# A fused attention, RWKV and expert kernel: attention chunks of 32 queries with two heads side by side, another place for the expert loads, two row buffers

## The chip, the cores and the metric

The kernel runs on one core of a Trainium2 chip. A core has TensorE (PE: matmuls; its weight loads are shown as PEld), VectorE (DVE), ScalarE (ACT), GpSimd (POOL) and SyncE (SP, which issues most DMAs). The metric is the device time of one execution in microseconds; less is better.

## The reference, cut

Three layers follow one another on 2 sequences of 768 tokens. The first is attention with 8 heads of 64, in chunks of 32 queries:

```python
chunk, left_ctx, right_ctx = (32, 16, 8)
for c in range(nc):
    l_start = max(0, c_start - left_ctx); r_end = min(S, c_end + right_ctx)
    k_full = np.concatenate([mem_k, k[:, :, l_start:r_end]], axis=2)   # 8 memory keys first
    scores = scale * np.matmul(q_c, k_full.transpose(0, 1, 3, 2))
    a = softmax(scores)
    out[:, :, c_start:c_end] = np.matmul(a, v_full)
```

So a chunk has at most 8 + 16 + 32 + 8 = 64 keys. The second layer (RWKV channel mixing) mixes each row of 512 with the row before it, and computes `r * v` with `k = relu(xk @ w_k)`, `v = k*k @ w_v`, `r = sigmoid(xr @ w_r)`. The third picks one of 8 experts for each token (a gate decides whether it keeps the expert of the token before), and gives `p[e] * (relu(x @ w1[e]) @ w2[e])`, with w1 512 x 1024 and w2 1024 x 512.

## The kernel before

**Units.** Tokens go in four units of 384. A unit has eight heads, that is four pairs; pairs are numbered 0 to 15 over all units, so pairs 0 to 3 belong to unit 0. The attention of unit u+1 runs between the RWKV matmuls of unit u. The first stage (0 to 98.6 us) is an exception: it splits the weights w_k, w_r and w_v into high and low parts on VectorE, ScalarE and GpSimd, does the attention of units 0 and 1, and the RWKV matmuls of unit 0. Its order is written by hand, as a table of step numbers (`ORDER`, `first_unit`). The later units are ordered by due times (`att_group`, `rwkv_block`, `route_*`).

**Attention.** A score group (`att_s`) is one head of one pair: two small matmuls of a mask from the constants tile `c_sb` (L359, L360), then six matmuls (L364), each of 64 queries against 96 keys, into one bank of PSUM. `att_max` (L372, L373) takes the maximum of each query, `att_exp` (L379) or `att_ex` (L389, first unit) the exponentials on ScalarE, `att_t` (L437) three transposes into a bank, and a copy makes `PT`. In the first stage `att_pvn` (L402) multiplies with the values, `att_nm` (L410 to L412) divides by the sum on VectorE, and `att_xt` (L418) transposes the result. From unit 2 on, `att_rc` (L428, L429) and `att_norm` (on GpSimd) divide before the transposes, and `att_pv` (L453) gives the result already transposed. There are two banks for scores, one (bank 5) for results, and two (6 and 7) for the router.

**RWKV and router.** The 128x384 matmuls of L514 to L516 are RWKV's (three for each product, of high and low parts). The router's matmuls are L602, L613, L645 (transposes of rows), L656 and L688. 

**Experts.** After the router, `tab_a` to `tab_e` (L976 to L1054) build tables of slots on VectorE: which tokens (`gix`, `six`), which expert (`ei`), and whether the slot's expert differs from the last one's. `tab_c` (L1020) multiplies with the last of them, `Rt` (L1008, L1009). A full slot has 128 tokens of one expert, a half slot 64. Full slots split the expert's weights into high and low parts (`w_part`, on ScalarE L863 and VectorE L866), and multiply: `tx` L906, `s1` L915 to L917, `th` L928, `s2` L937 to L939, `put` L942. Here there are 11 full slots (0 to 3, 4 to 7, 8, and 9 and 10 have one expert each), and a half slot follows on slots 3, 5, 7, 8 and 9 (L1111 to L1149), with weights of its own. `w_fetch(s, k)` (L885 to L887) loads the expert's w1 or w2 into the raw buffer if slot s begins a new expert; in the loop it is called as `w_fetch(s + 1, 1)` and `w_fetch(s + 2, 0)`. `h_fetch` (L1098, L1099) loads a half slot's weights. All of these loads are issued by SyncE, one after the other.

**Rows.** `put(s)` scales slot s's result into `ot[0]` on ScalarE; `store()` (L946), called in the next slot, writes it to DRAM by an indirect DMA with the indices `sixl`, which GpSimd copies. `half_rest` at the end is a nest of conditions for half slots that are left over; every engine walks through it.

Of the kernel before, what the change touches and what calls it, by code (L numbers as in the profile page):

```python
# [40 lines left out]
NSLOT = NFULL + NE  # L41
YW = DM + 1
NEGBIG = -float(2.0 ** 99)
# [24 lines left out]
)  # L68
BANKS = {"mm": (0, 1), "S": (2, 3), "pt": (4,), "x": (5,), "mi": (6, 7), "mm0": (0, 1, 6), "S0": (2, 3), "pt0": (4, 7)}


def first_unit_steps():
# [3 lines left out]
    room = dict(S=len(BANKS["S0"]), mm=len(BANKS["mm0"]), pt=len(BANKS["pt0"]), x=1, Pm=3, PT=4, tmp=4, dif=2, wcv=3)  # L76
# [5 lines left out]
    for n in range(8):  # L82
        step(f"qk{n}", "load_qk", (n,), [(DMA, 1.4, "")], (n > 5 and f"S{2 * n - 11}", n and f"qk{n - 1}"))
        step(f"v{n}", "load_v", (n,), [(DMA, 1.3, "")], (n > 2 and f"pv{n - 3}", n and f"v{n - 1}"))
    for n in range(8, 11):
        if n < 10:
            step(f"qk{n}", "load_qk", (n,), [(DMA, 1.4, "")], (f"S{2 * n - 11}", f"qk{n - 1}"))
        step(f"v{n}", "load_v", (n,), [(DMA, 1.3, "")], (f"pv{n - 3}", f"v{n - 1}"))
# [10 lines left out]
    for g in range(2 * H):  # L99
        n = g // 2  # L100
        step(f"S{g}", "att_s", (g,), [(PE, 0.8, "")], (f"qk{n}", f"S{g - 1}" if g else "cst"), take="S")
        step(f"mx{g}", "att_max", (g,), [(DVE, 0.65, "")], (f"S{g}",))
        step(f"ex{g}", "att_ex", (g,), [(ACT, 0.72, "")], (f"mx{g}",), take="Pm", give="S")
        step(f"t{g}", "att_t", (g,), [(PE, 0.33, "")], (f"ex{g}",), take="pt", give="Pm")
        step(f"pt{g}", "att_pt", (g,), [(ACT, 0.38, "a"), (DVE, 0.45, "d")], (f"t{g}",), take="PT", give="pt")
        if g % 2:
            step(f"pv{n}", "att_pvn", (n,), [(PE, 0.75, "")], (f"pt{g - 1}", f"pt{g}", f"v{n}", n and f"pv{n - 1}"),
                 take="x", give="PT PT")
            step(f"nm{n}", "att_nm", (n,), [(DVE, 0.85, "")], (f"pv{n}",), take="tmp", give="x")
            step(f"xt{n}", "att_xt", (n,), [(PE, 0.33, "")], (f"nm{n}",), take="pt", give="tmp")  # L110
            step(f"x{n}", "att_xc", (n,), [(ACT, 0.38, "a"), (DVE, 0.45, "d")], (f"xt{n}", n and f"x{n - 1}"), give="pt")
# [37 lines left out]
def kernel(  # L149
# [23 lines left out]
    banks = [psum.tile([P, 512], F32, name=f"bank{i}") for i in range(8)]  # L173
    turn = dict.fromkeys(BANKS, 0)
    spare = {}

    def bank(tag):

        if tag in spare:
            return banks[spare[tag].pop(0)]  # L180
        of = BANKS[tag]
        turn[tag] += 1
        return banks[of[turn[tag] % len(of)]]
# [36 lines left out]
    c_sb = cp.tile([P, 352], F32, name="c_sb")  # L220
# [9 lines left out]
    hi64 = c_sb[:, 136:137]  # L230
    pcol1 = c_sb[:, 158:159]
# [97 lines left out]
    NG = NU * H  # L329
    Sb, mxs, Pm, sm, PT, pts, xb = {}, {}, {}, {}, {}, {}, {}  # L330
    xT = {}

    def get_xT(u):
        if u not in xT:
# [7 lines left out]
    stock["Pm"] = [(ap_.tile([P, NTI, KW], F32, bufs=1, name=f"Pm{k}"), ap_.tile([P, NTI], F32, bufs=1, name=f"sm{k}"))  # L342
                   for k in range(3)]
    stock["PT"] = [ap_.tile([KW, UT], F32, bufs=1, name=f"PT{k}") for k in range(4)]

    def scores(g):
        return Sb[g][:, 0:NTI * KW].rearrange("p (i k) -> p i k", k=KW)

    def att_s(g):
        n, j = divmod(g, 2)  # L350
        Sb[g] = bank("S0" if g < 2 * H else "S")
        s3 = scores(g)


        o = 32 if n // (H // 2) % 2 == 0 else 64
        m = c_sb[o:o + NCK, 192:352].bitcast(BF16)
# [9 lines left out]
        if j == 1 and 8 <= n < NG // 2 - 2:  # L366
            load_qk(n + 2)
# [961 lines left out]
```

## Time and profile before

| what | value |
|---|---|
| median of 3 runs | 480.97 us (480.62 to 481.92) |
| profiled execution | 480.1 us, of it 478.3 us span of the instructions |
| PE busy | 443.8 us, 93% |
| DVE, ACT, POOL busy | 253.8 (53%), 201.2 (42%), 108.4 us (23%) |
| moved by DMA queues | 73.46 MB, mean 154 GB/s |

The span runs from the first to the last instruction of the profiled execution; 1.8 us lie outside. Busy shares are means over stages of different kinds, so they have to be read by stretches: the first stage to 98.6 us, three units of some 60 us to 283, the experts to 466, and the end.

### The profile page before, as it was taken

The page shows a single profiled execution, that of the slowest core. Times are in us where ns is not written, and L with a number is a line of the kernel's source. Part 1 is how long each engine was busy: PE and PEld are TensorE (multiplying, and loading weights), DVE is VectorE, ACT ScalarE, POOL GpSimd, SP SyncE. Part 2 cuts the span into 40 slices and gives each one's busy share as a digit, 9 for nine tenths or more (in the row PEclk, how much of TensorE's full clock was granted, in tenths as well). Part 3 has the DMA queues.
Part 4 walks back from the last instruction along what each step waited for, and adds up shares of the span by engine and source line. Part 5 has one row for each costly group of instructions (what it writes and reads, how often), then busy time and mean ns, then how long its engine had stood idle before and what let it go on. Part 6 is the DMA issues. An engine that isn't in the chain of part 4 may idle for free. (4 is left out here: it accounts for less than half of the span.)

```text
span 478.3 us, 8826 instructions
## 1 busy us (share of the span) xinstructions
PE 443.8 (93%) x3147; PEld 371.0 (78%) x3147; DVE 253.8 (53%) x659; ACT 201.2 (42%) x486; POOL 108.4 (23%) x121
## 2 busy tenths in 40 slices
PE   1898999999999999999999989998999999989990
PEld 1576899989899898999899967785687786757680
DVE  5999997754754448544960287115342115555120
ACT  2666895346442364422470431225342125555220
POOL 2124210114310144100331611310130120214030
PEclk9999999999999999999999999999899999999996
DMA  8998710102222011000192013999650787991020
GB/s 306 350 320 284 284 53 26 51 6 105 68 69 67 26 67 27 0 1 2 44 346 73 0 46 126 383 398 368 234 207 24 284 304 264 407 344 53 23 77 22
DMA packets 27582, 73.46 MB, mean 154 GB/s; under 512 B 3819, under 2 KB 3951, under 8 KB 27520
## 3 DMA queue, kind: packets, MB, share of 16 engines
q1 hardware_dynamic: 24704, 64.23, 38.0%
q0 software_dynamic: 2816, 8.47, 5.2%
q8 instruction: 30, 0.49, 0.4%
q14 instruction: 32, 0.26, 0.2%
HBM read 106.24 MB, written 6.69 MB: 236 GB/s over the span
## 5 line engine op out<-in xcount | busy, mean ns | idle before, releaser
L899 DVE TENSOR_TENSOR w<-bank,w 128x512 fp32r<-128x512 f32 x34 | 23.4, 688 | 73.6 <-ACTq L877 59.3
L514 PE MATMUL bank<-xkh,w 128*128 128x384 f32 x128 | 46.6, 364 | 0.0
L514 PE MATMUL bank<-k2h,w 128*128 128x384 f32 x128 | 44.8, 350 | 0.0
L866 DVE TENSOR_TENSOR w<-raw,w 128x512 fp32r<-128x512 f32 x56 | 35.8, 696 | 16.0 <-ACT w L863 15.6
L516 PE MATMUL bank<-xkh,w 128*128 128x384 f32 x128 | 43.8, 342 | 0.0
L515 PE MATMUL bank<-xkl,w 128*128 128x384 f32 x128 | 43.7, 342 | 0.0
L516 PE MATMUL bank<-k2h,w 128*128 128x384 f32 x128 | 43.0, 336 | 0.0
L515 PE MATMUL bank<-k2l,w 128*128 128x384 f32 x128 | 42.8, 335 | 0.0
L898 ACT ACTIVATE w<-bank 128x512 fp32r<-128x512 f32 x34 | 20.3, 597 | 49.0 <-PE bank L928 27.3
L207 POOL TENSOR_TENSOR k2l<-tmp,k2h 128x384 fp32r<-128x384 f32 x24 | 26.7, 1114 | 51.5 <-DVE k2h L204 29.4
L863 ACT ACTIVATE w<-raw 128x512 fp32r<-128x512 f32 x64 | 35.3, 620 | 4.5 <-DMA raw<-in_w_dram 4.1
L915 PE MATMUL bank<-w,w 128*128 128x512 f32 x88 | 36.1, 411 | 0.5 <-issue 0.5
L937 PE MATMUL bank<-w,w 128*128 128x512 f32 x88 | 36.4, 414 | 0.0
L939 PE MATMUL bank<-w,w 128*128 128x512 f32 x88 | 34.7, 394 | 0.0
L917 PE MATMUL bank<-w,w 128*128 128x512 f32 x88 | 34.5, 392 | 0.0
L916 PE MATMUL bank<-w,w 128*128 128x512 f32 x88 | 34.4, 391 | 0.0
L938 PE MATMUL bank<-w,w 128*128 128x512 f32 x88 | 34.4, 390 | 0.0
L379 ACT ACTIVATE Pm<-bank,mx 128x96 f32<-128x96 f32 x48 | 15.7, 338 | 26.7 <-DVE mx L373 26.7
L514 PEld LDWEIGHTS bank<-xkh,w 128*128 128x128 f32 x128 | 24.5, 191 | 2.8 <-issue 1.9
L364 PE MATMUL bank<-qk 64*64 64x96 f32 x384 | 26.7, 280 | 0.0
L573 DVE SCALAR_TENSOR_TENSOR yT<-yT,bank 128x384 f32<-128x384 f32 x16 | 8.9, 553 | 31.6 <-PE bank L516 31.6
L514 PEld LDWEIGHTS bank<-k2h,w 128*128 128x128 f32 x128 | 24.0, 188 | 0.9
(222 smaller groups left out, 1005.5 us busy)
## 6 DMA issues: line engine op xcount, KB each, us to landing
raw<-in_w_dram SPq DMA_DIRECT2D x36, 2048.0 KB
qk<-in_qkx_dram SPq DMA_DIRECT2D x16, 480.0 KB
vt<-in_vx_dram SPq DMA_DIRECT2D x16, 292.5 KB
w<-in_wk_dram SPq DMA_DIRECT2D x8, 512.0 KB
w<-in_wv_dram SPq DMA_DIRECT2D x8, 512.0 KB
ys<-yr SPq DMA_DIRECT2D x12, 256.0 KB
w<-in_wr_dram SPq DMA_DIRECT2D x4, 512.0 KB
raw<-in_w_dram SPq DMA_DIRECT2D x2, 1024.0 KB
```

Source lines behind the costliest of these rows:

```text
L207: (nc.vector if e == "d" else nc.gpsimd).tensor_tensor(out=o, in0=a, in1=b, op=op)
L514: nc.tensor.matmul(o[:, :UT], lhsT=wh, rhs=xh, start=first, stop=False)
L515: nc.tensor.matmul(o[:, :UT], lhsT=wh, rhs=xl, start=False, stop=False)
L516: nc.tensor.matmul(o[:, :UT], lhsT=wl, rhs=xh, start=False, stop=last)
L863: nc.scalar.activation(out=hi, in_=src, func=ACTF.Copy)
L866: lo_on.tensor_tensor(out=lo, in0=src, in1=hi.bitcast(F32), op=ALU.subtract)
L915: nc.tensor.matmul(pb, lhsT=xh[:, sl], rhs=wh, start=(c == 0), stop=False)
L916: nc.tensor.matmul(pb, lhsT=xh[:, sl], rhs=wl, start=False, stop=False)
L917: nc.tensor.matmul(pb, lhsT=xl[:, sl], rhs=wh, start=False, stop=(c == NC - 1))
L937: nc.tensor.matmul(pb, lhsT=hh[:, sl], rhs=wh, start=(c == 0), stop=False)
L938: nc.tensor.matmul(pb, lhsT=hh[:, sl], rhs=wl, start=False, stop=False)
L939: nc.tensor.matmul(pb, lhsT=hl[:, sl], rhs=wh, start=False, stop=(c == NF - 1))
```

## The change

1. Attention works on chunks of 32 queries with exactly 64 keys, laid out by the host, so that no mask is needed. Both heads of a pair go together: 24 matmuls of 64 rows and 32 columns for the scores, head j in bank j of a pair of banks `Sb` (2 and 3; there is one such pair), one maximum, six exponentials of 64 columns, three transposes, and 24 matmuls with the values (65 columns, the last gives the sum) into another pair of banks `xb` (5 and 6). All units divide after that product. There are two buffers each for `Pm` and `PT` (three and four before), and two banks instead of three for the first unit's RWKV. The loads grow from 480 to 576 KB (qk) and from 292.5 to 390 KB (vt) for a pair. `ORDER` is another table, and the step rules (`room`, `step`) are those of pairs.
2. `w_fetch` reads a table `nx` of the next expert, made by `tab_n`, and is called when the present expert's raw weights have been split: for the second expert between `h_fetch(0)` and `h_fetch(1)`.
3. `put(s)` writes `ot[s % 2]`, and VectorE copies the indices into `sixl[s % 2]`; half slots have a tile `oh` of their own; two stores stand at the end instead of one.
4. `half_rest` stands in a condition `nr` (from `tab_r`), which is 0 for this data.

```diff
-BANKS = {"mm": (0, 1), "S": (2, 3), "pt": (4,), "x": (5,), "mi": (6, 7), "mm0": (0, 1, 6), "S0": (2, 3), "pt0": (4, 7)}
+BANKS = {"mm": (0, 1), "pt": (4,), "mi": (7,), "mm0": (0, 1), "pt0": (4, 7)}
...
+    def tiles():
         for i in range(NTI):
             for j in range(2):
...
+                for c in range(P // CHUNK):
+                    yield i, j, i * (P // CHUNK) + c, slice(j * D, (j + 1) * D), slice(c * CHUNK, (c + 1) * CHUNK)
+
+    def att_s(n):
+        for i, j, b, rows, cols in tiles():
+            nc.tensor.matmul(scores[cols, j, i, :], lhsT=qk[n][rows, b * CHUNK:(b + 1) * CHUNK],
+                             rhs=qk[n][rows, UT + b * KW:UT + (b + 1) * KW], start=True, stop=True)
...
+    def att_pvn(n):
+        for i, j, b, rows, cols in tiles():
+            nc.tensor.matmul(xb[cols, j, i * (D + 1):(i + 1) * (D + 1)], lhsT=PT[n][rows, b * CHUNK:(b + 1) * CHUNK],
+                             rhs=vt[n][rows, b, :], start=True, stop=True)
...
+    def att_pair(n, t):
+        at(t, att_s, n)
+        at(t + 0.35, att_max, n)
+        at(t + 0.65, att_ex, n)
+        at(t + 3.0, att_t, n)
+        at(t + 3.2, att_pt, n)
+        at(t + 3.7, att_pvn, n)
+        at(t + 3.8, att_nm, n)
+        at(t + 4.7, att_xt, n)
+        at(t + 4.9, att_xc, n)
...
-        ev = nc.values_load(ei[0:1, 0, s:s + 1], engines=(ET.SP,), min_val=0, max_val=NE - 1)
-        fv = nc.values_load(ei[0:1, 1, s:s + 1], engines=(ET.SP,), min_val=0, max_val=1)
+        ev = nc.values_load(nx[0:1, 0, s:s + 1], engines=(ET.SP,), min_val=0, max_val=NE - 1)
+        fv = nc.values_load(nx[0:1, 1, s:s + 1], engines=(ET.SP,), min_val=0, max_val=1)
...
-        nc.scalar.activation(out=ot[0], in_=banks[2 + s % 2], func=ACTF.Copy, scale=yg[s % 3][:, DM:DM + 1])
...
+        nc.scalar.activation(out=ot[s % 2], in_=banks[2 + s % 2], func=ACTF.Copy, scale=yg[s % 3][:, DM:DM + 1])
+        nc.vector.tensor_copy(sixl[s % 2], six[:, s:s + 1])
...
-        (15.3, gather, 2),
+        (15.3, gather, 2), (15.35, tab_n), (15.4, tab_r),
...
+    banks_of["mi"] = (6, 7)
...
         w_part(s, 3)
-        w_fetch(s + 1, 1)
-        store()
-        nc.gpsimd.tensor_copy(sixl, six[:, s:s + 1])
+        if s > 1:
+            w_fetch(s, 1)
+        store((s - 1) % 2)
...
         w_part(s + 1, 1)
-        w_fetch(s + 2, 0)
+        if s > 0:
+            w_fetch(s + 1, 0)
...
     h_fetch(0)
+    w_fetch(0, 0)
+    w_fetch(0, 1)
     h_fetch(1)
     slots(1)
-    half_rest([s >= NMIN for s in HALF_AT].index(True))
-
-    store()
+    nr = nc.values_load(ei[0:1, 0, NSLOT + 2:NSLOT + 3], min_val=0, max_val=1)
+    with tc.If(nr):
+        half_rest([s >= NMIN for s in HALF_AT].index(True))
+
+    store(1)
+    store(0)
```

On TensorE in unit 1, before: the end of one pair's product, and the scores of the next head (`bank_69` is bank 5, `bank_66` bank 2, `bank_65` one of RWKV's).

```order
L453 MATMUL bank_69<-PT_112,vt_916 64x64
L453 MATMUL bank_69<-PT_114,vt_916 64x64
L359 LDWEIGHTS c_sb
L359 MATMUL bank_66<-c_sb 128x192
L360 LDWEIGHTS c_sb
L360 MATMUL bank_66<-c_sb 128x96
L364 MATMUL bank_66<-qk_603 64x96 x6
L514 MATMUL bank_65<-xkh_116,w_173 128x384
L515 MATMUL bank_65<-xkl_117,w_173 128x384
```

The same place after (here `bank_68` is the pair of banks 5 and 6, `bank_66` the pair 2 and 3, and `bank_69` is bank 7):

```order
L480 MATMUL bank_65<-xkl_115,w_530 128x384
L481 MATMUL bank_65<-xkh_114,w_530 128x384
L388 MATMUL bank_68<-vt_970,PT_106 32x65 x24
L363 MATMUL bank_66<-qk_794 32x64 x24
L621 MATMUL bank_69<-ident,r_uk_1358 8x128 x3
L621 MATMUL bank_68<-ident,r_uk_1358 8x128 x3
L479 MATMUL bank_64<-xkh_108,w_260 128x384
```

The mask is gone, product and scores are one group each for a pair, and the router's transposes (L656 before, L621 after) now stand right behind them, half of them into the bank pair of the product.

On VectorE, in the tables, before: the steps from the tokens' slots to the selection `Rt`.

```order
L995 TENSOR_REDUCE se_3090<-sl_3089 128x36
L996 TENSOR_TENSOR slot<-se_3090,Qall 128x12
L997 TENSOR_TENSOR hf<-slot,se_3090 128x12
L998 SCALAR_TENSOR_TENSOR se_3090<-se_3090,slot 128x12
L1000 TENSOR_TENSOR hf<-hf,se_3090 128x12
L1001 TENSOR_TENSOR slot<-slot,hf 128x12
```

The same steps after (L964 to L970), with those of `tab_n` (L1038 to L1047) and `tab_r` (L1027):

```order
L1038 CAST tmp_146<-ei 1x17
L964 TENSOR_REDUCE se_3300<-sl_3299 128x36
L1039 SCALAR_TENSOR_TENSOR tmp_146<-c_sb,tmp_146 1x17
L1041 TENSOR_TENSOR tmp_146<-ef,tmp_146 1x17
L965 TENSOR_TENSOR slot<-se_3300,Qall 128x12
L1040 TENSOR_SCALAR tmp_146<-tmp_146 1x17
L1047 SCALAR_TENSOR_TENSOR nx<-tmp_146 1x17
L966 TENSOR_TENSOR hf<-slot,se_3300 128x12
L967 SCALAR_TENSOR_TENSOR se_3300<-se_3300,slot 128x12
L1042 TENSOR_TENSOR tmp_147<-tmp_146 1x289
L969 TENSOR_TENSOR hf<-hf,se_3300 128x12
L1027 SCALAR_TENSOR_TENSOR hl<-c_sb,tot 1x8
```

The new steps stand between the old ones, ahead of `Rt`.

On SyncE, after: between the half slots' weights `raw_1` and `raw_2` now stands the load of the next full expert (`raw_0`).

```order
L1095 DMA raw_1_3417<-in_w_dram 128x8x512
L851 TENSOR_LOAD nx
L851 ISA x2
L852 TENSOR_LOAD nx
L852 ISA x2
L853 ISA
L853 DMA raw_0_2668<-in_w_dram 128x4x1024
```

Before, this load of w1 into `raw_0` (L887) comes behind both half slots' loads.

## Rows read from the trace of the kernel before

**Rows 1.** Windows: length, busy us (instructions) by engine, granted clock, DMA share, GB/s.

```profile
0.00:45.10 45.10, 30.59 (x287) 22.85 (x287) 38.72 (x88) 25.55 (x61) 11.73 (x18) 1.00 0.93 315
20.00:40.00 20.00, 17.65 (x161) 13.44 (x159) 19.23 (x46) 13.76 (x37) 4.09 (x5) 1.00 0.99 322
45.10:98.60 53.50, 53.35 (x441) 49.11 (x441) 46.46 (x103) 35.16 (x86) 7.92 (x8) 1.00 0.33 110
99.50:159.60 60.10, 60.10 (x500) 54.64 (x496) 32.03 (x104) 25.27 (x85) 14.96 (x17) 1.00 0.22 67
```

**Rows 2.** Timeline of TensorE in unit 1: start, us, line, operands, records.

```profile
101.86 0.85 PE L602 MATMUL bank<-yT,wg_sb 128*32 128x384 f32 x8
102.64 0.45 PE L514 MATMUL bank<-xkh,w 128*128 128x384 f32 x1
...
105.52 0.25 PE L359 MATMUL bank<-c_sb 4*128 4x192 bf16 x1
...
105.74 0.71 PE L364 MATMUL bank<-qk 64*64 64x96 f32 x12
106.39 0.66 PE L645 MATMUL bank<-ident,yT 128*128 128x128 f32 x4
106.80 0.42 PE L514 MATMUL bank<-xkh,w 128*128 128x384 f32 x1
...
118.60 0.92 PE L453 MATMUL bank<-PT,vt 96*64 96x64 f32 x24
119.45 0.25 PE L359 MATMUL bank<-c_sb 4*128 4x192 bf16 x1
...
120.32 0.44 PE L514 MATMUL bank<-xkh,w 128*128 128x384 f32 x1
```

**Rows 3.** TensorE's groups of lines from 45.1 to 98.6 us: busy us, mean ns.

```profile
L364 PE MATMUL bank<-qk 64*64 64x96 f32 x72 | 4.3, 251 | 0.0
L437 PE MATMUL bank<-ident,Pm 128*96 128x128 f32 x24 | 4.0, 276 | 0.0
L402 PE MATMUL bank<-vt,PT 96*64 96x65 f32 x96 | 3.7, 225 | 0.0
```

**Rows 4.** Groups of VectorE and ScalarE from 45.1 to 98.6 us, mean ns.

```profile
L372 DVE TENSOR_REDUCE mx<-bank 128x3 f32<-128x288 f32 x7 | 3.1, 449 | 0.4 <-PE bank L364 0.4
L412 DVE TENSOR_TENSOR tmp<-bank,rc 128x384 f32<-128x384 f32 x4 | 2.2, 557 | 0.1
L373 DVE TENSOR_SCALAR mx<-mx 128x3 f32<-128x3 f32 x7 | 1.7, 247 | 0.2
...
L389 ACT ACTIVATE Pm<-bank,mx 128x96 f32<-128x96 f32 x23 | 6.2, 345 | 0.5 <-DVE rc L410 0.4
```

**Rows 5.** Expert stage: TensorE's waits, the chain, ScalarE's timeline, two windows.

```profile
PE bank L1131 <- ACT hv L1124: 4.4, 2, 2.3
...
316.14 13.43 DMA raw<-in_w_dram
...
426.25 0.69 ACT L942 ACTIVATE ot<-bank,yg 128x512 f32<-128x512 f32 x1 [3.08 <-issue]
...
335.67:339.08 3.41, 3.41 (x21) 1.77 (x22) 0.69 (x3) 0.38 (x1) 0.00 (x0) 0.67 0.18 19
339.08:342.00 2.92, 2.92 (x24) 1.67 (x22) 0.31 (x1) 0.00 (x0) 0.00 (x0) 0.80 0.90 332
```

**Rows 6.** Timeline of the tables on VectorE, and the matmul behind them.

```profile
286.62 0.28 DVE L1036 TENSOR_TENSOR tmp<-SE,c_sb 1x136 f32<-1x136 f32 x1
286.83 0.28 DVE L1037 TENSOR_TENSOR tmp<-SE,c_sb 1x136 f32<-1x136 f32 x1
...
292.45 0.35 DVE L1009 TENSOR_SCALAR Rt<-ohs,c_sb 128x276 bf16<-128x276 f32 x1
...
292.87 0.95 PE L1020 MATMUL bank<-Rt,OHr 128*128 128x30 bf16 x36
```

**Rows 7.** Timeline of GpSimd at the end.

```profile
472.42 1.02 POOL L946 DMA_INDIRECT out_dram<-ot,sixl  x1 [9.82 <-issue]
```

More of the change, by code (lines that the diff above doesn't have):

```diff
@@ L171 @@
     ys = dram.tile([B * S + 1, YW], F32, name="ys")
-    banks = [psum.tile([P, 512], F32, name=f"bank{i}") for i in range(8)]
+    banks = []
+    for i in range(8):
+        if i in (2, 5):
+            two = psum.tile([P, 2, 512], F32, name=f"bank{i}")
+            banks += [two[:, 0], two[:, 1]]
+            Sb, xb = (two, None) if i == 2 else (Sb, two)
+        elif i not in (3, 6):
+            banks.append(psum.tile([P, 512], F32, name=f"bank{i}"))
     turn = dict.fromkeys(BANKS, 0)
+    banks_of = dict(BANKS)
     spare = {}
@@ L340, in get_xT @@
         return xT[u]
[L342 to L356, printed above, removed]
-        edge, mid = m[:, P:P + KW], m[:, P + KW:P + 2 * KW].unsqueeze(1).to_broadcast([NCK, NTI - 1, KW])
-        ie, im = (slice(0, 1), slice(1, NTI)) if o == 32 else (slice(NTI - 1, NTI), slice(0, NTI - 1))
-        nc.tensor.matmul(s3[:, im, :], lhsT=m[:, 0:P], rhs=mid, start=True, stop=False, skip_group_check=True)
-        nc.tensor.matmul(s3[:, ie, :], lhsT=m[:, 0:P], rhs=edge.unsqueeze(1), start=False, stop=False, skip_group_check=True)
-        x = qk[n][j * D:(j + 1) * D]
-        for b in range(NTU):
-            i, h = divmod(b, 2)
-            nc.tensor.matmul(s3[h * TQ:(h + 1) * TQ, i, :], lhsT=x[:, b * TQ:(b + 1) * TQ],
-                             rhs=x[:, UT + b * KW:UT + (b + 1) * KW], start=False, stop=True, skip_group_check=True)
-        if j == 1 and 8 <= n < NG // 2 - 2:
@@ new lines @@
+    stock["Pm"] = [ap_.tile([P, NTI, 2, KW], F32, bufs=1, name=f"Pm{k}") for k in range(2)]
+    stock["PT"] = [ap_.tile([P, UT], F32, bufs=1, name=f"PT{k}") for k in range(2)]
+    scores = Sb[:, :, 0:NTI * KW].rearrange("p j (i k) -> p j i k", k=KW)
+    def tiles():
+        for i in range(NTI):
+            for j in range(2):
+                for c in range(P // CHUNK):
[4 more added lines that the diff above has]
+                             rhs=qk[n][rows, UT + b * KW:UT + (b + 1) * KW], start=True, stop=True)
+        if 8 <= n < NPR - 2:
@@ L367, in att_s, with att_max @@
             load_qk(n + 2)
[L369 to L372 removed]
+    def att_max(n):
+        mx = ap_.tile([P, 2, NTI], F32, tag="mx", bufs=2, name=f"mx{n}")
+        mxs[n] = mx
+        nc.vector.tensor_reduce(out=mx, in_=scores, op=ALU.max, axis=AX)
         nc.vector.tensor_scalar(out=mx, in0=mx, scalar1=-SCALE, scalar2=None, op0=ALU.mult)
[L375 to L381 removed]
@@ L385, in att_ex @@
-    def att_ex(g):
-        mx, s3 = mxs.pop(g), scores(g)
-        Pm[g], sm[g] = stock["Pm"].pop(0)
-        for i in range(NTI):
-            nc.scalar.activation(out=Pm[g][:, i, :], in_=s3[:, i, :], func=ACTF.Exp, bias=mx[:, i:i + 1], scale=SCALE)
-        leave("S0", Sb[g])
-        del Sb[g]
+    def att_ex(n):
+        mx = mxs.pop(n)
+        Pm[n] = stock["Pm"].pop(0)
+        for j in range(2):
+            for i in range(NTI):
+                nc.scalar.activation(out=Pm[n][:, i, j, :], in_=scores[:, j, i, :], func=ACTF.Exp, bias=mx[:, j, i:i + 1],
+                                     scale=SCALE)
@@ L393 @@
     xn = {}
     def att_pvn(n):
-        xb[n] = bank("x")
-        for i in range(NTI):
-            for j in range(2):
-                for h in range(2):
-                    b = 2 * i + h
-                    o = (2 * i + j) * (D + 1)
-                    nc.tensor.matmul(xb[n][h * TQ:(h + 1) * TQ, o:o + D + 1], lhsT=PT[2 * n + j][:, b * TQ:(b + 1) * TQ],
-                                     rhs=vt[n][:, b, j, :], start=True, stop=True)
-        stock["PT"] += [PT.pop(2 * n), PT.pop(2 * n + 1)]
@@ L415, in att_xt, with att_t, att_pt @@
+    def att_t(n):
+        pts[n] = bank("pt0" if n < H else "pt")
+        for i in range(NTI):
+            nc.tensor.transpose(pts[n][:, i * P:(i + 1) * P], Pm[n][:, i].rearrange("p j k -> p (j k)"), ident)
+        stock["Pm"].append(Pm.pop(n))
+    def att_pt(n, e="a"):
+        PT[n] = stock["PT"].pop(0)
+        copy(e, PT[n], pts[n][:, :UT])
+        if n < H:
+            leave("pt0", pts[n])
+        del pts[n]
     def att_xt(n):
-        pts[n, "x"] = bank("pt0")
+        pts[n, "x"] = bank("pt0" if n < H else "pt")
@@ L727 @@
         if u > 1:
-            for i in range(H):
-                att_group(u * H + i, T - 20 + 2.0 * i, 1.0)
+            for i in range(H // 2):
+                att_pair(u * H // 2 + i, T - 19 + 4.0 * i)
             for c in range(NC):
@@ L765 @@
     six = cp.tile([P, NSLOT], I32, name="six")
-    sixl = cp.tile([P, 1], I32, name="sixl")
-    ei = cp.tile([1, 2, NSLOT + 2], I32, name="ei")
+    sixl = [cp.tile([P, 1], I32, name=f"sixl{k}") for k in range(2)]
+    ei = cp.tile([1, 2, NSLOT + 3], I32, name="ei")
     fsel = cp.tile([1, 1], I32, name="fsel")
+    nx = cp.tile([1, 2, NFULL], I32, name="nx")
     def open_right():
@@ L964 @@
     tot = cp.tile([P, 3], F32, name="tot")
+    ef = cp.tile([1, NSLOT + 3], F32, name="ef")
+    nfull = ef[:, NSLOT + 1:NSLOT + 2]
     def tab_a():
@@ L1082 @@
         ot[k] = ep.tile([P, DM], F32, name=f"ot{k}")
+    oh = ep.tile([P, DM], F32, name="oh")
     yh = [ep.tile([P, YW], F32, name=f"yh{k}") for k in range(2)]
@@ L1285, in _layout @@
     cst[:, 160:172] = np.arange(NT)[None, :]
-    for half in range(2):
-        m = np.zeros((NCK, 320), f)
-        m[:, 0:P] = np.repeat(np.eye(NCK), CHUNK, 1)
-        m[:, P:P + KW], m[:, P + KW:] = msk[half][:, 2 * half], msk[half][:, 1]
-        m16 = (m.view(np.uint32) >> 16).astype(np.uint16)
-        cst.view(np.uint16)[32 + 32 * half:32 + 32 * half + NCK, 384:704] = m16
     e = np.arange(NE)
```

204 lines of the change are left out of this document (81 added, 123 removed), and 37 rows, old and new, of the table ORDER.

## The prediction

> **What bounds the kernel now.** I read the busy time by stretches first, then the rows of TensorE where the change touches it. From 45.1 us on TensorE leaves nothing: it is busy 53.35 of 53.50 us up to 98.6 and 60.10 of 60.10 us in the next unit [rows 1]. There any TensorE time that is taken away shortens the run, until another engine is late. VectorE has 28 us free in that unit, so nothing else is near. Before 45.1 TensorE is busy for only 30.59 us; VectorE works 38.72 and the DMA engines 0.93 of the time, and from 20 to 40 us these two stand at 19.23 of 20.00 and 0.99 [rows 1]. There TensorE's work is not the bound; VectorE and the loads are. In the expert stage TensorE waits twice for a copy of ScalarE, 4.4 us in all, the longer time 2.3 [rows 5].
>
> **Attention of units 2 and 3 (eight pairs of heads, beside the RWKV matmuls of units 1 and 2).** Scale first. Four fp32 transposes of 128 columns take 0.41 us from start to start (106.39 to 106.80), 0.80 ns a column [rows 2]. The 12 records of L364, 96 columns each, would take 0.92 us in a row at that price; they take 0.65 (105.74 to 106.39). Two column halves side by side give 0.46 and a rest of 0.19. The eight records of L602 (384 columns, tiles of 32 columns) would take 2.46 and take 0.78 (101.86 to 102.64): four side by side give 0.61 and a rest of 0.17. So the trace shows four column tiles at work together, and about 0.18 us for entering and leaving.
>
> Before, a pair costs two score groups of 0.87 us (105.52 to 106.39, the mask included) with 0.10 more on the 128-column matmul behind each (the 0.44 us record at 120.32), one group of L453 at 0.85 (118.60 to 119.45) and two sets of three transposes at 0.31 (three quarters of the 0.41) [rows 2]: 1.94 + 0.85 + 0.62 = 3.41 us. After, the scores are 24 matmuls of 64 columns. They count as 48 records, since six matmuls of L364 count as twelve. That is 48 x 64 x 0.80 = 2.46 us in a row; four side by side 0.61, with the rest 0.79. The second product has 65 columns: 0.80. Two sets of transposes stay, one of weights and one of results: 0.62. Together 2.21, so 1.2 us less a pair, 9.6 for eight; I keep **9.2 us**, since one matmul behind each group may again be 0.05 longer. The bounds: tiles two at a time give 2 x 1.41 + 0.62 = 3.44, no gain; eight at a time give 2 x 0.49 + 0.62 = 1.60, 14.5 us. I take four, which is what L602 shows with the same width of 32 columns. Nothing shows matmuls on different halves of the rows together.
>
> What comes with it: VectorE loses two L428 and two L429, gains L410 to L412 (0.557 us for the last [rows 4]), and its maximum runs once over 384 columns; in a unit where it is busy for 32.03 of 60.10 us [rows 1] that costs nothing. GpSimd loses the 16 normalisations. The cover fails at one place in each of units 1 and 2, which the order shows: the second product of a pair, the next scores, and at once two router transposes, one of them into the results' second bank. TensorE must wait there until VectorE has emptied it: the 0.557 us and two short operations before it, about 0.9 us behind the product, less the 0.8 us of scores between, plus what is queued on VectorE. With one 0.56 us operation queued that is 0.7 us each time: **+1.5 us** for both, from 0 (VectorE free) to 4 (three queued each time).
>
> **First unit (0 to 98.6 us).** Between 45.1 and 98.6 us TensorE does six score groups (72 records of L364), eight sets of L437 and four second products (L402) [rows 3]. With the new forms: six groups of 0.97 become three of 0.79, eight sets of 0.31 become four; the product stays. That is 5.82 - 2.37 + 1.24 = 4.7 us. Before 45.1 VectorE decides: two maxima of 0.449 + 0.247 us a pair [rows 4] become one of 0.60 (by columns) + 0.25, 0.54 less; five pairs lie there: 2.7 us. The scores no longer wait for the mask, but nothing else was ready then, so I count nothing. Against this stand bigger loads: 96 KB more of queries and keys and 97.5 KB of values for each pair, ten pairs, 1.9 MB. At 315 GB/s [rows 1] that is 6.1 us if all of it delays VectorE's weight splitting, and nothing if it fits in gaps. The free 0.07 of 45.1 us holds 1 MB, and two pairs (0.4 MB) load later, where the share is 0.33; 0.5 MB is left, 1.6 us. The sum is -4.7 - 2.7 + 1.6, **-6 us** in round numbers, from -9 (loads free, tiles faster) to 0 (loads cost all; two-tile price).
>
> ScalarE's exponentials are six of 64 columns for a pair instead of six of 96 (0.345 us each [rows 4]), so at most as long. The chain maximum, exponentials, transposes now holds the one pair of score banks; its price is in the rivals.
>
> **Experts.** The first stop: ScalarE waits for the second expert's weights. Their load was issued at 316.14 and took 13.43 us [rows 5]. Now the load stands in SyncE's queue between the two half-slot loads, about 294 us, so even with twice 13.43 us it lands by 321, before 329.6, where the first load ended. Its queue holds behind it only the second half-slot's load, needed much later. This gives back 2.3 us. Behind the stop the clock was also lower: granted clock 0.67 over 3.41 us and 0.80 over the next 2.92 [rows 5], so (0.33 x 3.41) + (0.20 x 2.92) = 1.7 us. The second stop: at 426.25 ScalarE begins `put(9)` after 3.08 us of idleness [rows 5]; the view names no releaser, but by the code the copy writes the one row buffer, out of which the store of the slot before still reads. Two buffers remove the other 2.0 us. Each stop lies on TensorE's path with full stretches behind it, so all three count: -6.0. They are bounded by 0 and -6.0.
>
> Against it: `tab_n` and `tab_r`, a dozen small VectorE operations, stand before the last table operation in VectorE's order. That one started at 292.45, and TensorE's L1020 at 292.87 starts where it ends [rows 6]; so the margin is nil. Twelve operations at 0.21 us from start to start (286.62 to 286.83) are 2.5 us; the steps they stand between wait for one another, so part fits in. I take **1.5 us**, from 0 (all fits) to 2.5. Nothing else hides it. The extra VectorE copy of the indices and one more store at the end (1.02 us [rows 7]) stand against two engine branches skipped; 0, from -1 to +1. Sum of the stage: -6.0 + 1.5 = **-4.5**.
>
> **Sum** against the profiled execution of 480.1 us (span 478.3, 1.8 outside): -9.2 + 1.5 - 6 - 4.5 = -18.2, 461.9. The median of the runs is 0.9 above the profiled one, so **463 us**.
>
> **Rivals.** 1, *eight tiles at a time*: tiles on the upper and the lower half of the rows run together, since the two heads go to two banks. The records show only column tiles together, so neither for nor against. Pairs cost 1.60 (5.3 us more gain), and in the first unit 2.1 us more of TensorE's work goes, half of it usable: 463 - 6.3 = 457. Here the Trainium skill ("TensorEngine Tiling (Array Packing)", Key Properties and Gotcha 1) bears: tiles work independently of each other, and row tiles may do so if their results go to different banks. The chance of this rival would be higher by that rule than by the rows; no row here shows it.
>
> 2, *the loads take the first unit's gain*: the DMA share of 0.99 from 20 to 40 us speaks for it, the free TensorE before 45 against: 463 + 6 = 469.
>
> 3, *the early load and the second buffer do not do what they say*: the stops remain because ScalarE is held by something else (the splitting of weights in front of the copy in its queue). Then 6.0 comes back: 469.
>
> 4, *slower*: the scores have one pair of banks. If TensorE's next scores stand at the head of its queue while maximum and six exponentials (0.85 + 6 x 0.34 = 2.9 us) of the last pair still run, TensorE stands still for up to 2.9 us a pair; 16 pairs cost 46 us, and 463 + 46 = 509. It decides for slower from 18.2 / 2.9 = 6.3 pairs on; at ten pairs 492. Against it: 36 of the RWKV matmuls and more lie between two score groups in units 1 and 2, by the order; for it: in the first unit's opening they are dense.
>
> **How the numbers follow.** Chances: forecast 0.38, rival 1 0.34, rival 2 0.12, rival 3 0.08, rival 4 0.05, a wash of several 0.03. The range 454 to 470 us holds the first four with the bounds of the bank clash and the tables (+1.5 and +2.5 on 463, -3 on 457) and leaves out some 0.12. A change of 0.3% (1.4 us) is what a measurement here can tell. Faster are the first four and a bit of the rest: 0.91; same 0.03; slower 0.06.
>
> **What would show it.** The scores of a pair in units 2 and 3: 0.79 us four at a time, 0.49 eight, 1.4 two. The first unit: RWKV of unit 1 begins at about 93 us instead of 99.5; at 99 rival 2 holds. Stops at L1131's successor: gone, and no clock below full behind it, else rival 3. A new stop of some 1.5 us before L989 (the old L1020). Rival 4 shows as TensorE idle, released by ScalarE's exponentials, ahead of L363. The forecast is wrong if the stretches of units 2 and 3 are not shorter by 4 to 5 us each.

## The result, and the profile after

The changed kernel takes 462.56 us (median of 4 runs, 460.95 to 463.79). Its ratio to the kernel before is 0.963, with a 95% interval of 0.957 to 0.968. The forecast of 463 us was met, and its direction and range too. But it was met by errors that cancel, as the stages show. The table takes the starts of RWKV's matmuls and the end of the last matmul from the timelines of the two profiled executions (480.1 and 463.79 us; the second is the slowest of its four runs, so the stages add up to less gain than the medians show).

| stage | before | after | difference | forecast |
|---|---|---|---|---|
| to the first RWKV matmul of unit 1 | 99.58 | 93.11 | -6.5 | -6 |
| units 1 and 2 | 121.1 | 110.7 | -10.4 | -9.2 + 1.5 |
| RWKV of unit 3 | 49.5 | 49.4 | 0 | 0 |
| from there to the last matmul | 196.25 | 196.36 | +0.1 | -4.5 |
| behind the last matmul | 11.9 | 12.3 | +0.4 | 0 |

So the attention gave more than forecast, and the expert stage, in which two stops were removed, gave nothing.

The windows that answer to [rows 1], with the columns named there:

```profile
0.00:45.10 45.10, 20.91 (x480) 16.33 (x480) 38.04 (x79) 23.77 (x59) 10.51 (x17) 1.00 0.89 329
20.00:40.00 20.00, 12.68 (x315) 9.46 (x314) 19.01 (x40) 12.20 (x31) 6.32 (x5) 1.00 0.84 310
45.10:93.10 48.00, 47.43 (x610) 43.76 (x610) 45.08 (x92) 33.40 (x83) 10.05 (x10) 1.00 0.44 156
93.10:148.30 55.20, 54.20 (x652) 50.92 (x653) 31.01 (x92) 20.30 (x57) 9.06 (x9) 1.00 0.27 88
```

From 20 to 40 us VectorE is as full as before (19.01 of 20), while TensorE has 5 us less to do and the DMA engines are no longer at their limit. From 93.1 to 148.3 TensorE's busy time is 1.0 us short of the window: a new wait.

The waits of TensorE from 45 us on, the releaser behind the arrow, then us in all, times, the longest:

```profile
PE bank L872 <- DMA yg<-ys,gix: 2.4, 1, 2.4
PE bank L894 <- ACT xh L1108: 2.4, 5, 0.5
PE bank L621 <- DVE tmp L400: 2.0, 2, 1.0
PE bank L479 <- ACT tmp L499: 1.6, 1, 1.6
PE bank L621 <- DVE r_uk L602: 1.3, 1, 1.3
PE bank L989 <- DVE Rt L978: 0.5, 1, 0.5
```

The two waits of [rows 5] on ScalarE's `hv` are gone. In their place stand the gather of slot 2's rows (L872; in the kernel before, at L906, TensorE waited 0.7 us for it) and five waits of 0.5 us at L894, which the kernel before has not. The two at L621 on L400 are the shared bank of the prediction. The one at L479 lies at 45 us, in the first stage, and the one at L621 on `r_uk` was there before as well (L656, 1.3 us). The line of the gather before:

```profile
PE bank L906 <- DMA yg<-ys,gix: 0.7, 1, 0.7
```

The timeline of TensorE in unit 1 that answers to [rows 2] (L388 is the product with the values, L363 the scores):

```profile
130.61 0.73 PE L388 MATMUL bank<-vt,PT 64*32 64x65 f32 x48
131.14 0.71 PE L363 MATMUL bank<-qk 64*32 64x64 f32 x48
131.78 0.44 PE L479 MATMUL bank<-k2h,w 128*128 128x384 f32 x1
```

The scores take 0.64 us from start to start, product and scores together 1.17; the forecast was 0.79 and 0.80. Both lie between my prices for four and for eight tiles at a time.

The expert stage behind the gather, with the columns of [rows 1], and the end on GpSimd:

```profile
286.80:289.20 2.40, 2.40 (x8) 2.11 (x9) 0.66 (x1) 0.60 (x1) 0.00 (x0) 0.51 1.02 405
289.20:292.00 2.80, 2.80 (x11) 2.22 (x11) 0.19 (x2) 0.18 (x1) 0.00 (x0) 0.81 1.03 375
...
452.60 1.02 POOL L913 DMA_INDIRECT out_dram<-ot,sixl  x1 [9.28 <-ACTq L1209]
456.74 1.00 POOL L913 DMA_INDIRECT out_dram<-ot,sixl  x1 [3.12 <-DMA out_dram<-ot,sixl]
```

Behind the gather's wait the granted clock is 0.51 of full, the lower of its two levels (1.2 GHz), for 2.4 us, and 0.81 for the next 2.8: 0.49 x 2.4 + 0.19 x 2.8 = 1.7 us, just what the removed stop cost in [rows 5]. At the end the second store stands still for 3.12 us until the first has landed, though they write different rows.

The sum of the expert stage is then: -4.4 (the two stops), 1.7 of clock lost at another place instead of 1.7 won, +1.7 (the gather's 2.4 instead of 0.7), and +2.7 for the five places of L894. The wait behind the tables (L989, 0.5) stands against one of the same length at L915 in the kernel before. The sum is 0.0, where 0.1 was measured.

### The profile page after: what moved, and what is told of

The parts are those of the page before. It is cut to its first block, busy times and chain, and to the rows that moved or that the text cites. A ratio compares the mean times of both kernels' runs of the same rounds, so it can differ in the third digit from the quotient of the medians.

```text
span 461.9 us, 10044 instructions
## 1 busy us (share of the span) xinstructions
PE 415.2 (90%) x3827; PEld 351.1 (76%) x3827; DVE 252.1 (55%) x637; ACT 187.4 (41%) x425; POOL 95.5 (21%) x97
## 5 line engine op out<-in xcount | busy, mean ns | idle before, releaser
L479 PE MATMUL bank<-xkh,w 128*128 128x384 f32 x128 | 46.5, 363 | 1.9 <-ACT tmp L499 1.6
L479 PE MATMUL bank<-k2h,w 128*128 128x384 f32 x128 | 44.6, 348 | 0.0
L381 ACT ACTIVATE Pm<-bank,mx 128x64 f32<-128x64 f32 x96 | 21.4, 323 | 21.9 <-DVE mx L372 21.3
L505 ACT ACTIVATE tmp<-bank 128x384 f32<-128x384 f32 x24 | 11.9, 495 | 41.2 <-PE bank L481 37.5
L479 PEld LDWEIGHTS bank<-xkh,w 128*128 128x128 f32 x128 | 24.6, 192 | 5.0 <-ACT tmp L499 2.3
L480 PEld LDWEIGHTS bank<-xkl,w 128*128 128x128 f32 x128 | 24.6, 192 | 1.4 <-DVE xkl L211 1.4
L481 PEld LDWEIGHTS bank<-xkh,w 128*128 128x128 f32 x128 | 24.5, 191 | 0.0
```

The source lines that it names most:

```text
L479: nc.tensor.matmul(o[:, :UT], lhsT=wh, rhs=xh, start=first, stop=False)
L480: nc.tensor.matmul(o[:, :UT], lhsT=wh, rhs=xl, start=False, stop=False)
L481: nc.tensor.matmul(o[:, :UT], lhsT=wl, rhs=xh, start=False, stop=last)
```

## The experiments

The runs come in sets, each with runs of the kernel before, whose median lies between 477.9 and 480.8 us from set to set. So each time below is followed by its ratio to the kernel before of the same set, with the 95% interval; the changed kernel has 0.963 (0.957 to 0.968). A difference of 2 or 3 us between two kernels is clear in the traces and not in these ratios.

**Five waits of 0.5 us at L894.** L894 transposes in bank 5 for a full slot; L1107, just ahead, transposes a half slot's rows in bank 6, and ScalarE copies these out. No data passes between them, but the change has made one tile of banks 5 and 6.

```diff
     def h_tx(h):
-        pb = banks[6]
+        pb = banks[7]
```

> The changed kernel, with the half slots' input transposes (h_tx) in bank 7 instead of bank 6. In the trace of the changed kernel TensorE waits five times for 0.47 us at L894 (th, bank 5), released by ScalarE's copy of h_tx's bank 6; before there was no such wait. Theory: banks 5 and 6 are now one tile, so the transposes of L894 wait for a copy that doesn't concern them; a half slot's place costs 0.54 us, five make 2.7 us. Then the five waits vanish and the time falls by 2.7 us, to about 460. Rival: the wait is real (ScalarE is late, or bank 5 itself is not free); then the five waits of 0.47 stay, and the time is unchanged.

The waits are gone; what is left of the list from the gather down:

```profile
PE bank L872 <- DMA yg<-ys,gix: 1.9, 1, 1.9
PE bank L479 <- ACT tmp L499: 1.4, 1, 1.4
PE bank L621 <- DVE r_uk L602: 1.3, 1, 1.3
```

The last matmul ends at 446.59 instead of 449.62: 3.0 us, of which 0.5 is the shorter wait for the gather. The median is 460.97 us (0.964 of before, 0.960 to 0.968); by the ratios the two kernels can't be told apart, by the traces they can. So the wait came from the common tile alone, and it cost about what five times 0.54 us say.

**How many tiles work together.** Two orders of the same 24 matmuls. In the changed kernel four of one head alternate with four of the other.

```diff
-        for i in range(NTI):
-            for j in range(2):
+        for j in range(2):
+            for i in range(NTI):
                 for c in range(P // CHUNK):
```

> The changed kernel with the 24 matmuls of scores and of the second product in another order: all twelve of head 0, then all twelve of head 1, so that neighbours in the queue lie on the same half of the rows. Measured so far: 0.65 us for a group, between my estimates for four tiles at a time (0.79) and for eight (0.49). Theory A: tiles on both halves of the rows do overlap, and the order in the queue limits it; then a group costs about 0.79 here, 0.13 more, and units 1 and 2 (16 groups) 2.1 us more, the first unit up to 1 us more. Theory B: the rate of the queue (10 ns a matmul) limits, whatever tiles are used; then a group costs 0.65 as before and the time is the same.

```profile
131.09 0.78 PE L388 MATMUL bank<-vt,PT 64*32 64x65 f32 x48
131.67 0.76 PE L363 MATMUL bank<-qk 64*32 64x64 f32 x48
132.36 0.44 PE L479 MATMUL bank<-k2h,w 128*128 128x384 f32 x1
```

The scores take 0.69 us here, 0.05 more; product and scores 1.27 instead of 1.17. Units 1 and 2 take 111.5 us instead of 110.7. The median is 464.11 us (0.970, 0.965 to 0.976).

```diff
         for i in range(NTI):
-            for j in range(2):
-                for c in range(P // CHUNK):
+            for c in range(P // CHUNK):
+                for j in range(2):
```

> The changed kernel with the two heads alternating matmul by matmul, so that neighbours in the queue lie on different halves of the rows. Theory A (halves overlap, the order limits): a group falls towards 0.49 us, 16 groups in units 1 and 2 give up to 2.6 us back. Theory B (the rate of the queue limits): 0.65 as before, no change.

```profile
130.71 0.73 PE L388 MATMUL bank<-vt,PT 64*32 64x65 f32 x48
131.24 0.71 PE L363 MATMUL bank<-qk 64*32 64x64 f32 x48
131.88 0.45 PE L479 MATMUL bank<-k2h,w 128*128 128x384 f32 x1
```

0.64 us, as in the changed kernel, 463.05 us (0.969, 0.964 to 0.973). Neither theory fits whole. Order matters, which speaks for an overlap of the two halves of the rows, but it is worth 0.05 us and not 0.13. And with the heads apart a group is still quicker than four at a time by my price. Of the 48 single records of the product the first eight start within 46 ns and the next eight follow from 80 ns on; with the heads apart only four start within 20 ns, and the next four follow from 81 ns on. Behind some 33 records one starts about every 13 ns (17 with the heads apart). That may be a limit of supply, and not of tiles; what limits it was not tried. The Trainium skill ("TensorEngine Tiling (Array Packing)", Key Properties and Gotcha 1) has tiles on different rows run together if they write to different banks. The eight starts within 46 ns agree; a whole group, at 0.64 us, does not reach my price for eight at a time, 0.49.

**The gather of slot 2.** Issued at 278.60, it lands at 286.74, 8.1 us later, beside loads that fill the DMA engines.

```diff
+    gw = dram.tile([1, 4], F32, name="gw")
+    nc.sync.dma_start(out=gw, in_=yg[2][0:1, 0:4])
     h_fetch(0)
     w_fetch(0, 0)
```

> The changed kernel, in which SyncE waits for the gather of slot 2's rows (a tiny transfer that reads them) before it issues the big loads of half slots and the next expert. In the trace of the changed kernel the gather is issued at 278.60 and TensorE waits for it 2.41 us, until 286.78, beside loads that hold the DMA engines at 0.99; the granted clock is 0.51 for 2.4 us behind it. Theory: the gather is slow because it shares the engines with the loads; alone it takes some 4 us, the wait and the low clock vanish, and the time falls by 2.4 + 1.6 = 4 us, unless the loads that now start 4 us later make a wait of their own. Rival: the gather takes its 8 us by itself (indices, descriptors); then the wait stays, and the later loads cost up to 8 us of their own or nothing.

The waits of TensorE from 275 us on:

```profile
PE bank L1127 <- ACT hv L1120: 7.3, 1, 7.3
PE bank L894 <- ACT xh L1108: 2.4, 5, 0.5
PE bank L989 <- DVE Rt L978: 0.5, 1, 0.5
```

The wait at L872 is gone: alone, the gather lands 3.6 us after its issue (278.81 to 282.44), before TensorE comes. But the loads now start at 286.06 instead of 278.30, and ScalarE begins to split the second expert's weights 8.3 us late: 468.99 us (0.980, 0.976 to 0.984). The theory of the gather holds, and the prediction's stop is back, in another place of the same chain. ScalarE's and SyncE's lines there:

```profile
317.86 2.19 ACT L829 ACTIVATE w<-raw 128x512 fp32r<-128x512 f32 x4 [8.26 <-DMA raw<-in_w_dram]
...
SPq L853 <- DMA raw<-in_w_dram: 4.8, 1, 4.8
```

The w1 that ScalarE needs is not what is late: it was issued at 288.67 and had landed by 308.57, and ScalarE was ready at 309.60. By the semaphores of the trace ScalarE waits for a later `w_fetch` into the same buffer, which loads nothing since the expert stays the same, but which SyncE passes only at 317.72. Ahead of it in SyncE's queue stands a fetch into w2's buffer, and that one waits 4.8 us until the second expert's w2 has landed, at 315.51.

**The shared bank of the results.**

```diff
-            yt, bt, ct = ((2.02, 3.02, 4.02), 5.02, 7.02) if u < NU - 2 else ((3.02, 4.02, 5.02), 2.02, 3.52)
+            yt, bt, ct = ((2.02, 3.02, 4.02), 6.02, 7.02) if u < NU - 2 else ((3.02, 4.02, 5.02), 2.02, 3.52)
```

> The changed kernel with the router's step route_b due one block later in units 0 and 1, so that its two transposes (L621) stand behind the block of RWKV matmuls and the transposes of the pair (L419), and not right behind second product and scores. In the trace of the changed kernel TensorE waits 1.00 us twice at L621, released by VectorE's L400, which empties the second bank of the product. Theory: it is the shared bank and nothing else; both waits vanish, units 1 and 2 shorten by 1.0 us each, 2 us in all. Rival: the wait moves to the next user of the bank (L653, which now follows sooner behind the scan of VectorE), and nothing is won.

```profile
PE bank L653 <- DVE r_ukt L630: 4.8, 4, 2.1
```

The rival came out: L621 no longer waits, but L653 waits 2.1 us in each of the two units, and the clock falls behind it:

```profile
118.30:125.30 7.00, 7.00 (x77) 6.43 (x80) 3.94 (x16) 1.88 (x4) 2.00 (x2) 0.51 0.04 3
179.70:183.40 3.70, 3.70 (x60) 3.26 (x60) 2.60 (x10) 1.19 (x3) 1.10 (x1) 0.54 0.06 0
```

470.81 us (0.983, 0.978 to 0.988). In the trace units 1 and 2 take 117.6 us instead of 110.7. Of these 6.8 us only 2.2 are the longer waits; the rest is the lower clock, which by these rows cost about 0.49 x 7.0 + 0.46 x 3.7 = 5 us. Moved the other way, two blocks earlier, the step costs nothing (the run with four mends, below).

**The early loads undone.**

```diff
-        ev = nc.values_load(nx[0:1, 0, s:s + 1], engines=(ET.SP,), min_val=0, max_val=NE - 1)
+        ev = nc.values_load(ei[0:1, 0, s:s + 1], engines=(ET.SP,), min_val=0, max_val=NE - 1)
...
-        if s > 1:
-            w_fetch(s, 1)
+        w_fetch(s + 1, 1)
...
-    w_fetch(0, 0)
-    w_fetch(0, 1)
```

> The changed kernel with the expert loads where they were before: w_fetch reads the old table, is called one slot ahead, and stands behind both half slots' loads (the new tables are still made). Theory of the prediction: ScalarE waits for the second expert's weights again and TensorE stops behind slot 3 for some 2.3 us or more (the stage is entered earlier, loads are not), with a lower clock behind it: +2.3 + 1.7 = +4 us there. The gather of slot 2 is then beside the half slots' loads alone. If the early loads are what slows the gather, its wait (2.41 us) falls towards the 0.66 of before and the net is near +1.5; if the half slots' loads alone do, it stays, and the net is +4.

463.44 us (0.968, 0.962 to 0.975), the last matmul at 449.43: the same as with early loads, where either outcome of the expectation was slower. ScalarE does wait again,

```profile
314.28 2.20 ACT L829 ACTIVATE w<-raw 128x512 fp32r<-128x512 f32 x4 [1.06 <-DMA raw<-in_w_dram]
...
319.51 0.37 ACT L1120 ACTIVATE hv<-bank 128x256 f32<-128x256 f32 x1
...
319.93 0.44 PE L1127 MATMUL bank<-ident,hv 128*128 128x128 f32 x2
```

but its `hv` ends at 319.88, when TensorE has just finished what stands ahead of L1127. The reading: TensorE had lost just enough in front of that place (clock and L894) that the late weights were in time. It is tried below. The gather's wait is 1.9 us here, so the half slots' loads alone are enough for it.

**One row buffer again.**

```diff
-        nc.scalar.activation(out=ot[s % 2], in_=banks[2 + s % 2], func=ACTF.Copy, scale=yg[s % 3][:, DM:DM + 1])
-        nc.vector.tensor_copy(sixl[s % 2], six[:, s:s + 1])
+        nc.scalar.activation(out=ot[0], in_=banks[2 + s % 2], func=ACTF.Copy, scale=yg[s % 3][:, DM:DM + 1])
...
-        store((s - 1) % 2)
+        store(0)
+        nc.gpsimd.tensor_copy(sixl[0], six[:, s:s + 1])
...
-    store(1)
     store(0)
```

> The changed kernel with one row buffer again (put writes ot[0], GpSimd copies the one index tile behind each store, one store at the end). Theory: the stop in front of the last half slot comes back, ScalarE's put waits for the store of the slot before, some 2.0 us at L1127, and the end is shorter by the second store, up to 1 us: net +1 to +2. Rival: the store is no longer in the way since the loads lie elsewhere; then no stop, and the time is the same or 0.4 less.

459.10 us (0.959, 0.953 to 0.966), two runs. No stop came back, as the rival has it, and behind the last matmul there are 9.1 us of span instead of 12.3, with one store at the end. The last matmul ends at 447.79, 1.8 us earlier: behind a wait of 1.9 us for the gather the clock did not fall in this run.

```profile
286.45:288.90 2.45, 2.45 (x13) 2.10 (x14) 0.69 (x1) 0.60 (x1) 0.46 (x2) 1.00 1.04 408
```

The store in front of the last half slot holds GpSimd's next copy back for 5.3 us instead of the 6.7 of the kernel before, and that is enough for ScalarE. Why this store is quicker stays open. The 1.8 us are not the buffer's: in two runs with both buffers in which the clock did not fall either (the heads alternating, and the stores at once below) the last matmul ends at 447.86 and 447.73.

**As many bytes again in the first stage.**

```diff
         nc.sync.dma_start(out=qk[n], in_=qkx[u, hp])
+        if n < 10:
+            xl = dram.tile([P, 387], F32, name=f"xl{n}")
+            nc.sync.dma_start(out=xl, in_=qkx[u, hp][:, 0:387])
```

> The changed kernel with one more transfer of 198 KB for each of pairs 0 to 9, behind its queries and keys (a copy from DRAM to DRAM that nothing uses): as much again as the change has added to a pair's loads, 2 MB in all. It prices the loads in the first stage, in which RWKV of unit 1 starts at 93.1 us. If the first stage is bound by loads, the start moves by about 2 MB / 0.32 MB per us = 6 us, to 99, and the change's own 1.9 MB cost as much; if loads fit in gaps, by less than 1 us; my sum took 1.6.

```profile
93.63 0.44 PE L482 MATMUL bank<-xkh,w 128*128 128x384 f32 x1 [0.18 <-DVE yT L541]
```

RWKV of unit 1 starts at 93.63 instead of 93.11 (462.18 us, 0.966, 0.959 to 0.973). In the other nine kernels that leave the first stage as it is the start lies between 93.00 and 93.55, so 2 MB cost 0.5 us at most. So the first stage was not bound by its loads, and the change's own 1.9 MB probably cost less than the 1.6 us of my sum; taking them away was not tried.

**Four mends together.** (a) is the first experiment; the rest:

```diff
-            yt, bt, ct = ((2.02, 3.02, 4.02), 5.02, 7.02) if u < NU - 2 else ((3.02, 4.02, 5.02), 2.02, 3.52)
+            yt, bt, ct = ((2.02, 3.02, 4.02), 3.52, 7.02) if u < NU - 2 else ((3.02, 4.02, 5.02), 2.02, 3.52)
...
-    h_fetch(0)
-    w_fetch(0, 0)
-    w_fetch(0, 1)
-    h_fetch(1)
+    gw = dram.tile([1, 4], F32, name="gw")
+    w_fetch(0, 0, gw)
+    w_fetch(0, 1)
+    h_fetch(0)
...
         slot_body(s)
         if s == 1:
+            h_fetch(1)
...
         put(s)
+        store(s % 2)
...
-    store(1)
-    store(0)
```

> The changed kernel with four things mended. (a) h_tx in bank 7: the five waits of 0.47 us at L894 go (-2.7). (b) route_b due two blocks before the product of the pair (3.52 instead of 5.02): the two waits of 1.0 us on the shared bank go without the wait at the router's next step that the later place had (-2.0). (c) SyncE waits for the gather of slot 2's rows just before the first big load, loads the second expert first, the first half slot's weights next, and those of the second half slot only after slot 1: the gather's wait of 1.9 to 2.4 us goes, and no wait for weights comes (-2, and -1.6 where the clock fell). (d) each slot's rows are stored right behind its put, and no store stands at the end: the span behind TensorE's last matmul falls from 12.3 us to below 9.1, the value with one store (-3 or more). Sum: 462.6 - 10 to 12 = 451 to 453. If the stage's gains again vanish into waits further on, the waits of ScalarE on raw weights or of TensorE at L1127 will show it.

456.04 us (0.950, 0.947 to 0.954). Of the waits, the ones at L872, L894 and the shared bank are gone; the last matmul ends at 442.53, 7.1 us earlier, although the clock fell in the router's stage (0.51 from 266.5 to 270.0 us, 1.7 us), where it had stayed full in the changed kernel. But 13.2 us follow it, so (d) failed and the sum of 451 to 453 was missed. Alone:

> The changed kernel with (d) alone: each slot's rows are stored behind its put, none at the end. In the trace of the changed kernel the last but one store is issued at 452.60 and the last waits for it until 456.74; with one buffer and one store at the end the span behind the last matmul was 9.1 us, with two 12.3. Theory: the second store at the end costs 3.2 us; here none is left, so 462.6 - 3.2 = 459.4 or less. Rival: GpSimd's walk through the skipped branches sets the end (before, the one store was issued 6.0 us behind the last matmul); then 0 to -1.

```profile
448.74 1.02 POOL L913 DMA_INDIRECT out_dram<-ot,sixl  x1 [9.17 <-ACT ot L908]
```

462.77 us (0.965, 0.960 to 0.970). The last store is issued 1.0 us behind the last matmul (447.73) and yet the span ends 12.3 us behind it. After the store GpSimd still walks through the skipped branches, and does so only when the store has landed: its next semaphore operation for the store (L1210) comes at 452.47, 3.7 us behind the issue, the walk ends at 455.94, and the closing of the program takes the last 4.1 us. The rival was right.

**Early or late loads once the rest is mended.** (a) and (b) as above and the stores of (d), the loads as in the kernel before, with the gather awaited ahead of the first half slot's and the second half slot's behind slot 1.

> The kernel with the four mends, but with the expert loads one slot ahead and behind the half slots' loads as in the kernel before. In the changed kernel with late loads alone no stop came back; my reading is that TensorE had been made 2.2 us later in front of it by the gather's wait, the lower clock and the wait at L894, so that the late weights were just in time. Here those are gone: the stop at L1127 behind slot 3 should be back with some 2 us, with or without a lower clock behind it (1.6): +2 to +4 on the run with four mends. If there is no stop, the early loads are worth nothing in this kernel and the reading is wrong.

```profile
PE bank L1129 <- ACT hv L1122: 7.3, 1, 7.3
...
321.10:325.00 3.90, 3.88 (x18) 2.00 (x18) 1.02 (x3) 0.38 (x1) 1.02 (x1) 0.50 0.25 72
```

465.70 us (0.971, 0.966 to 0.976), the last matmul at 451.15 against 442.53: 8.6 us. The stop is back and larger than 2 us: TensorE comes to this place 6.1 us earlier than with late loads alone (313.85 instead of 319.93), and `hv` ends 1.2 us later (321.06), since the half slots' loads start later here. So the reading holds: late loads cost nothing while TensorE is held up in front of that place, and 8.6 us when it is not. The two kernels compared here differ in the order of all the big loads, though, and not only in early or late; that early loads alone do not prevent the stop shows in the run that only awaited the gather.

**The best version.** Mends (a) to (c), one row buffer, one store at the end.

> The kernel with mends (a) to (c) of the four, and in place of (d) one row buffer and one store at the end, as in the kernel before (the condition around the rest of the half slots stays). With four mends TensorE's last matmul ended at 442.5 us but 13.3 us of span followed: GpSimd's skipped branches come after the last store and wait for it. With one buffer and one store at the end that rest was 9.1 us. Theory: the rest is 9.1 again, so 456.0 - 4 = 452, less what the single buffer costs: ScalarE's put waited 0.6 us for the store in front of the last half slot when TensorE had been held up 0.5 us at L894; here it isn't held, so a stop at L1127 of up to 0.5 us may come back in this place. 452 to 453. If the second buffer is worth the 2.0 us of the prediction, it is 454.

453.03 us (0.944, 0.940 to 0.948); against the changed kernel's 462.56, 9.5 us less (9 by the ratios). TensorE's waits from 200 us on, of 0.3 us or more:

```profile
PE bank L621 <- DVE r_uk L602: 1.3, 1, 1.3
...
PE bank L816 <- DVE R L813: 0.5, 1, 0.5
PE bank L991 <- DVE Rt L980: 0.5, 1, 0.5
...
PE bank L653 <- DVE r_ukt L630: 0.3, 1, 0.3
```

There is no stop at the last half slot. The last matmul ends at 441.81, and 9.4 us follow.

## Why the prediction came out, step by step

- *Attention of units 2 and 3*, -9.2: right in kind, too small. A pair has 1.17 us of product and scores where I took 1.59. Measured: -10.4 with 2.0 of new waits in it, so -12.4. The step that failed is "I take four": the row of L602 shows four tiles on the full height, and the halves of the rows overlap besides. Rival 1 was half right: eight start together, but the product takes 0.53 us and the scores 0.64, and not 0.49.
- *The shared bank*, +1.5: +2.0, two waits of 1.00 at L621 on VectorE's L400. The first of them was at the place that the order shows.
- *First unit*, -6: -6.5. At 45.1 us TensorE had 24 of RWKV's matmuls behind it instead of 18, some 1 us at 0.17 each; the other 5.4 us came behind that point, where 4.7 were forecast. The loads, put at 1.6 us, cost at most some 0.5 if the experiment with as many bytes again is taken for them, so this term was too dear, and VectorE's 2.7 must then have been too large; the two were not measured apart. Rival 2 was refuted: the start came at 93.1 us, not at 99.
- *Experts*, -4.5: +0.1. The two stops left as forecast, and so far rival 3 was wrong: the second expert's w1 was issued at 280.90 and had landed by 302.4. The step that failed is "all three count". Three things that I had not priced took their place: the gather of slot 2, which came 0.7 us late before and 2.4 now; the lower clock behind that wait; and the common tile of banks 5 and 6, which I followed only as far as the router. Behind `tab_n` and `tab_r` TensorE waits 0.5 us (L989) and not 1.5.
- *Second row buffer*, part of these -4.5: with one buffer there is no stop either, in two kernels. The 2.0 us that I gave it were not its own; what took that stop away was not tried apart from the early loads and the new attention.
- *The end*, 0: +0.4. By the run with one buffer the second store costs 3.2 us (12.3 against 9.1), and the skipped branches gave 2.8 back (9.1 against 11.9).
- *Rival 4*, a stop at the scores: no wait at L363 on exponentials stands in the list from 45 us on, and ahead of that L363 waits for its loads alone (10.5 us), so it did not come.

So the time was right by luck, because 3.2 us more from attention and 0.5 more from the first unit stood against 4.6 us that the experts did not give, 0.5 more at the shared bank and 0.4 at the end: -16.4 us of span where -18.2 were forecast. The mechanism was right in the attention and, as far as it was measured, in the first unit, and wrong in the experts.

## What to carry to other kernels

When a wait is removed, ask what else stands in the same chain: here the new waits, ahead of the first stop's place, covered it, so undoing the early loads cost nothing until those waits were mended, and 8.6 us then. The second row buffer was worth nothing in any run. When buffers are joined into one tile, list all users of every part, in all stages, since each becomes a wait on the others. And a forecast that is met should still be held against its stages.

## What the runs showed that I had not expected

A wait of about 2 us of TensorE may cost its own length alone or 1.7 us more (once 3.4), and its length does not tell which. Behind the wait for the gather the clock fell in the changed kernel (wait 2.41 us), with h_tx in bank 7 (1.95), with the heads apart (1.98) and with the late loads (1.89); it stayed at full with one row buffer (1.94), with the stores at once (1.92), with the heads alternating (2.02) and with the extra loads (2.14). The windows behind it with h_tx in bank 7, with the late loads and with the stores at once, with the columns of [rows 1]:

```profile
286.80:291.30 4.50, 4.50 (x15) 3.54 (x14) 0.85 (x2) 0.60 (x1) 0.00 (x0) 0.62 1.00 371
287.00:291.50 4.50, 4.50 (x15) 3.50 (x14) 0.84 (x2) 0.70 (x2) 0.00 (x0) 0.62 1.02 381
286.45:290.95 4.50, 4.50 (x22) 3.80 (x23) 0.85 (x2) 1.29 (x2) 0.07 (x1) 1.00 1.04 403
```

Where the clock fell it cost 0.38 x 4.5 = 1.7 us each time, as in [rows 5]. The waits of 1.0 us (L621) left the clock at full; the second stop of the kernel before (2.04 us) did too, and two waits of 2.09 us (L653) lowered it, the first for twice as long. What decides was not tried. So single traces of the expert stage can differ by 1.7 us for this alone.

A store at the end of the program is not free of what stands behind it on its queue: the 12.3 us behind the last matmul were the same with the last store issued 7.1 us behind it and 1.0 us behind it.
